# Attention and two dense layers on one core: opening transposes on TensorE, a third buffer for weight pieces, empty rows added behind the second tile of keys

## The chip, the cores and the metric

The kernel runs on one core of one Trainium2 chip. The metric is the device time of one execution in microseconds (us), lower is better. Three runs of the kernel before gave a median of 734.42 us (733.02 to 736.55). Engines are named as the profile names them: PE is TensorE (PEld its weight loads), DVE VectorE, ACT ScalarE, POOL GpSimd, SP the engine that issues nearly all DMAs here.

## The reference

```python
# attention: B, H, S, D = 2, 8, 768, 64; 16 clusters a head
q_assign = argmax(q_n @ c_n.T); k_assign = argmax(k_n @ c_n.T)    # q_n, k_n, c_n: normalised rows
mask = q_assign[:, :, :, None] == k_assign[:, :, None, :]
scores = np.where(mask, q @ k.T / sqrt(D), -1e9)
attn = softmax(scores) @ v                          # 16 (batch, head) pairs
x = attn.transpose(0, 2, 1, 3).reshape(1536, 512)
h = x @ w_in;  x = softplus(h) @ w_out              # layer 1: 512 -> 2048 -> 512
h = x @ w_in2; x = leaky_relu(h, 0.01) @ w_out2     # layer 2
```

The weights come as float64 and are decoded on the chip. Products that need more than half precision are split into high and low halves of 16 bits.

## The kernel before

The 16 (batch, head) pairs are called heads 0 to 15, and each has 768 rows in C = 6 tiles of 128. The work of one head is a chain through all engines:

- `load` fetches q and k (two DMAs). `split` makes 16-bit high and low halves: ACT casts into `nq` (L293) and copies (L295), POOL subtracts (L294). The halves in `n1` are then transposed by one DMA from SP into `t` (L297): 12 blocks of 128x128.
- `assign_mm` multiplies `t` with the transposed centroids `ct` (24 small matmuls, L306); `assign_el` finds each row's cluster on DVE (L319 to L325) and ACT writes the one-hot columns beside the data in `nq` (L328, L329). A second DMA transpose from SP makes `tq` of it (L331, 12 blocks).
- `emit_s1` computes all masked scores once for the row maxima: 12 matmuls (L345), each with a DVE maximum (L352). `emit_m` joins the maxima (L359), PE turns them by a diagonal matmul (L366), and ACT copies them into rows 96 to 127 of `tq` (L374).
- `emit_s2` computes the scores again, 2 times 6 pairs of matmuls (L392, L393), ACT exponentiates (L399), POOL makes the low half (L401); `emit_pv` multiplies with v into one PSUM tile `x` (L428, L429, L433, or L415 for the second tile of keys of heads 0 to 7). `emit_empty` adds, with six matmuls of 32 rows (L451) that read `tq` and `svr` (column sums of v, `emit_sv`), what rows without any key of their cluster get. `emit_norm` divides (L470 to L476).

Beside this, `w_piece` loads 512 KB pieces of the layer-1 weights into `st` (L153, two buffers), DVE decodes them in three steps (L140, L143, L146), ACT and DVE make the halves (L162, L163). From head 8 on, layer-1 matmuls (L697, L710) fill PE between the heads; after the attention, from about 315 us, only layer work is left, and layer 2 (L562) ends the program.

A scheduler places the instructions of every engine in one fixed order when the program is built, by priorities (`at_pri`) and its own estimate of times. At run time each engine takes its instructions strictly in that order, so an instruction that waits holds back all that stand behind it on its engine, and SP holds back DMAs in the same way. Buffer counts decide waits too: `BUFS` gives, for each tile name, buffers in the late pool and extra ones for heads 0 to 7. `tq` has 3 and 1, so the transpose into `tq` of head h in the second half waits for the last reader of `tq` of head h-3, which is its `emit_empty`. `behind_tk(h)` puts an instruction behind head h's `tq` transpose on SP.

Of the kernel before, what the change touches and what calls it, by code (L numbers as in the profile page):

```python
# [8 lines left out]
F32 = mybir.dt.float32  # L9
# [15 lines left out]
BUFS = {  # L25
# [4 lines left out]
}  # L30
# [14 lines left out]
FF_PRI, FF_STEP, FF_RATE = 8, 0.25, 0.75  # L45

W_FREE, W_FROM, W_TO, W_PER = 4, 8, 10, 5
W_PRI = ((0, 0.5), (17, 0.3))
# [8 lines left out]
def attn_moe_kernel(  # L57
# [93 lines left out]
    def w_piece(dsth, dstl, src):  # L151
        st = wst.tile([128, 512, 2], I32, tag="st", name="st")
        nc.sync.dma_start(out=st, in_=src.rearrange("p (n t) -> p n t", t=2))  # L153

        def conv(bank=False):
            if bank:
                c = pm.tile([128, 512], I32, tag="m0", name="wcp")
            else:
                c = wst.tile([128, 512], I32, tag="wc", name="wc")
            decode(c, st)  # L160
            cf = c.bitcast(F32)
            S.activation(out=dsth, in_=cf, func=AF.Copy, scale=WS)  # L162
            V.scalar_tensor_tensor(out=dstl, in0=cf, scalar=WS, in1=dsth, op0=ALU.mult, op1=ALU.subtract)  # L163

        return conv
# [117 lines left out]
    def split_v(h):  # L283
        vv, v2 = v_t.pop(h), v2s[h % V_BUFS]
        S.copy(out=v2[:, :, D:2 * D], in_=vv)
        ENG[by_group(VLO, h)].tensor_tensor(out=v2[:, :, 0:D], in0=vv, in1=v2[:, :, D:2 * D], op=ALU.subtract)

    def split(h):
        qk = ld_t.pop(h)
        n_ = n_of[h]  # L290
        n1 = atile([128, C, 4, D], F16, "n1", h)
        for t_ in range(2):
            S.copy(out=n_[:, t_, :, 0:D], in_=qk[:, t_])  # L293
            G.tensor_tensor(out=n1[:, :, 1 + t_, :], in0=qk[:, t_], in1=n_[:, t_, :, 0:D], op=ALU.subtract)  # L294
            S.copy(out=n1[:, :, 3 * t_, :], in_=n_[:, t_, :, 0:D])  # L295
        t = atile([128, 2 * C, 128], F16, "t1", h)
        nc.sync.dma_start_transpose(out=t, in_=n1.rearrange("p c s d -> p (c s d)"))  # L297
        tp1[h] = t
# [15 lines left out]
    def assign_el(h):  # L314
# [15 lines left out]
        t = atile([128, 2, C, 128], F16, "tq", h)  # L330
        tki[h] = nc.sync.dma_start_transpose(  # L331
            out=t.rearrange("p t c r -> p (t c) r"), in_=n_.rearrange("p t c d -> p (t c d)")
        )
        tp2[h] = t[:, 0], t[:, 1]
# [71 lines left out]
    def emit_pv(h, kt):  # L406
# [5 lines left out]
        if pl is None:  # L412
            pf = p.rearrange("p a r -> p (a r)")
            for c in range(C):
                PE.matmul(  # L415
                    out=xps[:, c * XW:(c + 1) * XW],
                    lhsT=pf[:, c * 128:(c + 1) * 128],
                    rhs=v32s[h % V_BUFS][:, kt, :],
                    start=(kt == 0 and c == 0),
                    stop=False,  # L420
                )
            return
# [7 lines left out]
        for c in range(C):  # L430
            cs = slice(c * 128, (c + 1) * 128)
            o = xps[:, c * XW:(c + 1) * XW]
            PE.matmul(out=o, lhsT=pl[:, cs], rhs=v2[:, kt, D:2 * D + 1], start=False, stop=False)  # L433

# [13 lines left out]
    def emit_empty(h):  # L448
        t, r, xps = tpq[h], svs.pop(h), x_t[h]
        for c in range(C):  # L450
            PE.matmul(out=xps[:, c * XW:(c + 1) * XW], lhsT=t[MR:KS2, c, :], rhs=r[MR:KS2, :], start=False, stop=(c == C - 1))  # L451

# [284 lines left out]
    nc.sync.dma_start(out=cn, in_=cen.rearrange("h c d -> (h c) d"))  # L737
    load(0)
    sq = acon.tile([128, D], F32, name="sq")
    ss = acon.tile([128, 4], F32, name="ss")  # L740
    c16 = acon.tile([128, 4, D], F16, name="c16")
    with at_pri(-9):
# [13 lines left out]
        centred = V.tensor_tensor(out=c16[:, 2:4, :], in0=two, in1=c16[:, 0:2, :], op=ALU.subtract)  # L756
        nc.sync.dma_start_transpose(out=ct, in_=c16.rearrange("p s d -> p (s d)"))
    load(1)
# [10 lines left out]
    for v2 in v2s:  # L769
        G.memset(v2[:, :, 2 * D:2 * D + 1], 1.0)  # L770
    G.memset(ones, 1.0)
    G.affine_select(
        out=ident, in_=ones, pattern=[[1, 128]], compare_op=ALU.is_equal, fill=0.0, base=0, channel_multiplier=-1
    )
    G.memset(ones[:, MR:MR + C], 0.0)
# [119 lines left out]

    def chain(h):
        if h < NH:
            with at_pri(h - LEAD_SPLIT):
                split(h)
            with at_pri(h - LEAD_ASSIGN):  # L900
                assign_mm(h)
                assign_el(h)
            with at_pri(h - LEAD_MAX):
                for c in range(C):
                    emit_s1(h, c)
            if h + 2 < NH:
                with at_pri(h - LEAD_LOAD):
                    load(h + 2)
# [8 lines left out]
    st = {"credit": 0.0}  # L917
    for h in range(AHEAD):
        chain(h)
    split_v(0)  # L920
    for h in range(NH):
# [14 lines left out]
        for j in range(C):  # L936
            with at_pri(h + j / 6):
                emit_s2(h, j)
                if j:
                    emit_pv(h, j - 1)  # L940
            if h < H - 1 and (j + h * C) % W_PER == 0:
                w_step()
# [4 lines left out]
        with at_pri(h + 1):  # L947
            emit_pv(h, C - 1)
            emit_empty(h)
        with at_pri(h + 1 - LEAD_NORM):  # L950
# [50 lines left out]
```

## Time and profile before

| | us |
|---|---|
| median of 3 runs (device time) | 734.42 |
| the profiled execution, device time | 732.15 |
| its span in the trace | 730.4 |
| PE busy / DVE / ACT / POOL in it | 677.0 / 517.3 / 410.9 / 402.5 |
| idle time of PE before its first matmul | 11.72 |

The profile names an instruction by its line, engine, operation and tiles (`tq<-nq` reads `nq` and writes `tq`). Busy time is the union of an engine's instructions. What ended a wait is shown behind an arrow: `<-DMA tq<-nq` is the landing of that DMA. SP's rows (SPq) show how long the issue of a DMA took there, not the transfer. The granted clock of PE is a share of full speed (1.00 is 2.4 GHz, 0.50 is 1.2 GHz).

### The profile page before, as it was taken

The page shows a single profiled execution, that of the slowest core. Times are in us where ns is not written, and L with a number is a line of the kernel's source. Part 1 is how long each engine was busy: PE and PEld are TensorE (multiplying, and loading weights), DVE is VectorE, ACT ScalarE, POOL GpSimd, SP SyncE. Part 2 cuts the span into 40 slices and gives each one's busy share as a digit, 9 for nine tenths or more (in the row PEclk, how much of TensorE's full clock was granted, in tenths as well). Part 3 has the DMA queues.
Part 4 walks back from the last instruction along what each step waited for, and adds up shares of the span by engine and source line. Part 5 has one row for each costly group of instructions (what it writes and reads, how often), then busy time and mean ns, then how long its engine had stood idle before and what let it go on. Part 6 is the DMA issues. An engine that isn't in the chain of part 4 may idle for free. (4 is left out here: it accounts for less than half of the span.)

```text
span 730.4 us, 18968 instructions
## 1 busy us (share of the span) xinstructions
PE 677.0 (93%) x7584; PEld 506.7 (69%) x7584; DVE 517.3 (71%) x1167; ACT 410.9 (56%) x1087; POOL 402.5 (55%) x494
## 2 busy tenths in 40 slices
PE   1798899998889899999999999999999999999997
PEld 1367677665656566656666566558999999999996
DVE  4797798998898782069787867965585757575545
ACT  5476666768878753355245425526555555565553
POOL 6387777778888864303324233325556465565653
PEclk9999999999999999999999999999999999999999
DMA  8985966766565632013322355787000000000000
GB/s 204 221 173 113 181 136 122 170 123 173 129 161 152 141 116 53 2 35 103 110 93 82 108 175 193 235 304 261 3 31 2 30 2 7 27 2 31 2 31 30
DMA packets 104521, 77.87 MB, mean 107 GB/s; under 512 B 78320, under 2 KB 92656, under 8 KB 104432
## 3 DMA queue, kind: packets, MB, share of 16 engines
q1 hardware_dynamic: 104288, 76.40, 40.4%
q8 instruction: 59, 0.97, 0.5%
q14 instruction: 30, 0.25, 0.1%
q10 hardware_dynamic: 144, 0.26, 0.1%
HBM read 50.36 MB, written 10.49 MB: 83 GB/s over the span
## 5 line engine op out<-in xcount | busy, mean ns | idle before, releaser
L401 POOL TENSOR_TENSOR pl<-p 128x768 f16<-128x768 f32 x88 | 128.3, 1468 | 56.3 <-ACT p L399 36.0
L352 DVE TENSOR_REDUCE mm<-s 128x1 f32<-128x384 f32 x190 | 100.6, 548 | 19.3 <-PE s L345 16.7
L562 PEld LDWEIGHTS <-w_in2h 128*128 128x128 f16 x1344 | 98.2, 98 | 5.3 <-issue 0.7
L570 DVE TENSOR_TENSOR gl<-r,gh 128x384 f16<-128x384 f32 (+1 forms) x96 | 63.2, 659 | 50.0 <-ACT gh L608 49.3
L697 PE MATMUL m<-xt,w_inh 128*128 128x384 f16 x512 | 93.8, 326 | 4.2 <-ACT rl L521 3.4
L399 ACT ACTIVATE p<-s 128x384 f32<-128x384 f32 x160 | 74.2, 492 | 30.9 <-PE s L393 28.3
L710 PE MATMUL m<-g_l,w_outh 128*128 128x384 f16 x256 | 83.4, 326 | 2.0 <-DVE g_l L511 1.9
L710 PE MATMUL m<-g_h,w_outh 128*128 128x384 f16 x256 | 83.5, 326 | 0.0
L710 PE MATMUL m<-g_h,w_outl 128*128 128x384 f16 x256 | 83.3, 326 | 0.0
L570 POOL TENSOR_TENSOR r<-r,r 128x128 f32<-128x128 f32 x95 | 47.8, 520 | 55.5 <-ACT r L600 55.2
L697 PEld LDWEIGHTS <-w_inh 128*128 128x128 f16 x512 | 49.7, 98 | 38.7 <-issue 6.1
L608 ACT CAST gh<-r 128x384 f16<-128x384 f32 (+1 forms) x96 | 54.2, 565 | 36.6 <-POOL r L570 33.6
L710 PEld LDWEIGHTS <-w_outh 128*128 128x128 f16 x512 | 49.8, 98 | 32.5
L345 PE MATMUL s<-tq 128*128 128x384 f16 x190 | 62.0, 345 | 9.3 <-DMA tq<-nq 4.5
L562 PEld LDWEIGHTS <-gh 128*128 128x128 f16 x672 | 60.5, 98 | 6.4 <-issue 1.1
L200 POOL TENSOR_TENSOR wd<-wd 128x256 f32<-128x256 f32 x32 | 29.3, 925 | 53.9 <-DVE sg L194 39.2
L562 PE MATMUL i<-xt,w_in2h 128*128 128x128 f16 x576 | 57.2, 219 | 0.1
L392 PE MATMUL s<-t 128*128 128x384 f16 x160 | 53.2, 333 | 3.1 <-ACT p L399 2.3
L393 PE MATMUL s<-tq 128*128 128x384 f16 x160 | 53.2, 333 | 1.6 <-ACT tq L374 1.6
L562 PE MATMUL i<-sh,w_in2h 128*128 128x128 f16 x384 | 53.5, 219 | 0.4 <-ACT r L600 0.4
L562 PE MATMUL i<-sl,w_in2h 128*128 128x128 f16 x384 | 53.5, 219 | 0.0
L562 PE MATMUL i<-sh,w_in2l 128*128 128x128 f16 x384 | 53.4, 219 | 0.0
(145 smaller groups left out, 1861.1 us busy)
## 6 DMA issues: line engine op xcount, KB each, us to landing
st<-in_moe_w_in_dram SPq DMA_DIRECT2D x32, 512.0 KB, 4.6
st<-in_moe_w_out_dram SPq DMA_DIRECT2D x32, 512.0 KB, 3.7
kept<-sg SPq DMA_DIRECT2D x16, 256.0 KB, 2.8
qk<-in_q_dram SPq DMA_DIRECT2D x16, 192.0 KB, 3.5
qk<-in_k_dram SPq DMA_DIRECT2D x16, 192.0 KB, 3.7
v<-in_v_dram SPq DMA_DIRECT2D x16, 192.0 KB, 4.7
kept<-sg SPq DMA_DIRECT2D x24, 128.0 KB, 2.7
out_dram<-ob SPq DMA_DIRECT2D x11, 256.0 KB, 2.0
```

Of the source, the lines that this page charges most:

```text
L200: G.tensor_tensor(out=out, in0=in0, in1=in1, op=ALU.subtract)
L345: PE.matmul(out=o, lhsT=t[:, c, :], rhs=tk[:, 3 * j:3 * j + 3, :], start=True, stop=True,)
L352: V.reduce_max(out=mms[h % 2][:, c, j:j + 1], in_=bank[:, 0:3 * 128], axis=AX)
L392: PE.matmul(out=o, lhsT=t1[:, kt, 1, :], rhs=t1[:, 3 * j:3 * j + 3, 0, :], start=True, stop=False)
L393: PE.matmul(out=o, lhsT=t2[:, kt, :], rhs=tqh[:, 3 * j:3 * j + 3, :], start=False, stop=True)
L399: S.activation(out=p[:, j, :], in_=sp, func=AF.Exp, scale=scale)
L401: G.tensor_tensor(out=pl, in0=p, in1=pb, op=ALU.subtract)
L562: one = PE.matmul(out=bank, lhsT=w_, rhs=x_, start=(first and i == 0), stop=(i == len(ops) - 1), skip_group_check=True)
L570: eng.tensor_tensor(out=out, in0=in0, in1=in1, op=op)
L608: S.copy(out=gh[:, lo:hi], in_=r[:, lo:hi])
L697: PE.matmul(out=hp, lhsT=w_, rhs=x_, start=(i == 0), stop=(i == len(ops) - 1))
L710: PE.matmul(out=yp, lhsT=w_[:, kk, ms], rhs=g_[:, kk, :], start=(n == 0), stop=(n == 3 * KFF - 1))
```

## The change

1. The transposes of `ct`, of `t` for heads 0 and 1, and of `tq` for head 0 are done by PE: matmuls of each 128x128 block against `ident`, up to four to a PSUM bank, copied out by ACT and DVE in turn. In the program these are 38 matmuls, 7 ACT casts and 3 DVE casts more, and 4 DMA transposes fewer. `ident` is made at the beginning.
2. The first two heads are written stage by stage instead of head by head, and on SP the `t` transposes of heads 3 and 4 and the loads of those heads stand behind `tq` transposes of earlier heads.
3. Weight pieces of layer 1 get a third `st` buffer, in the attention's pool; for it, `t` has one early buffer less (5 in all for heads 0 to 7) and `y` has one buffer instead of two.
4. `emit_empty(h)` stands behind the second tile of keys instead of behind the last (with the flags that close the accumulation moved to the last tile's matmuls).

```diff
-    "qk": (2, 1), "n1": (1, 2), "t1": (4, 2), "tq": (3, 1),
+    "qk": (2, 1), "n1": (1, 2), "t1": (4, 1), "tq": (3, 1),
...
-    "dd": (2, 0), "y": (2, 0), "xn": (2, 0),
+    "dd": (2, 0), "y": (1, 0), "xn": (2, 0),
...
+EMPTY_AT = 2
+PE_HEADS = 1
+OPENING = (3, 4)
+ST_MORE = 1
...
     def w_piece(dsth, dstl, src):
-        st = wst.tile([128, 512, 2], I32, tag="st", name="st")
+        n = turn["st"] = (turn.get("st", -1) + 1) % (2 + ST_MORE)
+        st = (wst if n < 2 else at).tile([128, 512, 2], I32, tag="st", name="st", bufs=2 if n < 2 else ST_MORE)
...
+    def pe_transpose(out, in_, blocks, odd=False):
+
+        for i in range(0, blocks, 4):
+            m = min(4, blocks - i)
+            if odd and i == 8:
+                bank = pm.tile([128, 512], F32, tag="m0", name="m")
+            else:
+                bank = ring("as" if blocks <= 4 else "s1" if odd else "s2", 0)
+            for j in range(m):
+                cs = slice((i + j) * 128, (i + j + 1) * 128)
+                PE.matmul(out=bank[:, j * 128:(j + 1) * 128], lhsT=in_[:, cs], rhs=ident, start=True, stop=True)
+            to = out[:, i:i + m].rearrange("p i r -> p (i r)")
+            if i % 8 == 0:
+                S.copy(out=to, in_=bank[:, 0:m * 128])
+            else:
+                V.tensor_copy(out=to, in_=bank[:, 0:m * 128])
...
-        nc.sync.dma_start_transpose(out=t, in_=n1.rearrange("p c s d -> p (c s d)"))
+        if h <= PE_HEADS:
+            pe_transpose(t, n1.rearrange("p c s d -> p (c s d)"), 2 * C, h == 1)
+        else:
+            with behind_tk(h - 2 if h in OPENING else -1):
+                nc.sync.dma_start_transpose(out=t, in_=n1.rearrange("p c s d -> p (c s d)"))
...
+        if h < PE_HEADS:
+            pe_transpose(to, from_, 2 * C)
+        else:
+            tki[h] = nc.sync.dma_start_transpose(out=to, in_=from_)
...
-        nc.sync.dma_start_transpose(out=ct, in_=c16.rearrange("p s d -> p (s d)"))
+        pe_transpose(ct, c16.rearrange("p s d -> p (s d)"), 2)
...
-                with at_pri(h - LEAD_LOAD):
+            if h + 2 < NH and "m" in parts:
+                with at_pri(h - LEAD_LOAD), behind_tk(h - 1 if h + 1 in OPENING else -1):
                     load(h + 2)
...
-    for h in range(AHEAD):
-        chain(h)
+    for parts in "sam":
+        for h in range(AHEAD):
+            chain(h, parts)
...
                 if j:
                     emit_pv(h, j - 1)
+                if j == EMPTY_AT:
+                    emit_empty(h)
...
             emit_pv(h, C - 1)
-            emit_empty(h)
```

Three places show what the new order does. The first is SP from the centroids' transpose on (before), where `t` and `tq` are the outputs of the two DMA transposes of a head and `qk` its loads:

```order
L757 DMA_TRANSPOSE ct<-c_112 128x2x128
L297 DMA_TRANSPOSE t_176<-n_169 128x12x128
L297 DMA_TRANSPOSE t_261<-n_254 128x12x128
L273 DMA qk<-in_q_dram 128x384
L274 DMA qk<-in_k_dram 128x384
L297 DMA_TRANSPOSE t_360<-n_353 128x12x128
L273 DMA qk<-in_q_dram 128x384
L274 DMA qk<-in_k_dram 128x384
L331 DMA_TRANSPOSE tq<-nq_85 128x12x128
L297 DMA_TRANSPOSE t_662<-n_655 128x12x128
L331 DMA_TRANSPOSE tq<-nq_86 128x12x128
```

And the same stretch of SP in the changed kernel, down to the first weight piece:

```order
L323 DMA_TRANSPOSE t_414<-n_407 128x12x128
L361 DMA_TRANSPOSE tq<-nq_86 128x12x128
L278 DMA qk<-in_q_dram 128x384
L279 DMA qk<-in_k_dram 128x384
L323 DMA_TRANSPOSE t_716<-n_709 128x12x128
L278 DMA qk<-in_q_dram 128x384
L279 DMA qk<-in_k_dram 128x384
L278 DMA qk<-in_q_dram 128x384
L279 DMA qk<-in_k_dram 128x384
L361 DMA_TRANSPOSE tq<-nq_87 128x12x128
L158 DMA st<-in_moe_w_in_dram 128x1024
```

Four transposes are gone from the head of the queue; the first weight piece (`st`) still stands behind the `tq` transpose of head 2 (`nq_87`), as it does before.

The second place is DVE ahead of the first decode of a weight piece (`wcp<-st`); `mm_96` are the maxima of head 1 and `as`, `m`, `mx`, `oh` the cluster search, here of head 3. Before:

```order
L359 TENSOR_REDUCE dg_102<-mm_95 128x6
L352 TENSOR_REDUCE mm_96<-s_300 128x1
L361 TENSOR_SCALAR dg_102<-dg_102 128x6x2
L352 TENSOR_REDUCE mm_96<-s_303 128x1
L319 TENSOR_REDUCE mx<-as 128x12
L352 TENSOR_REDUCE mm_96<-s_306 128x1
L320 TENSOR_TENSOR as<-as,mx 128x192
L321 TENSOR_TENSOR as<-as,tab 128x192
L352 TENSOR_REDUCE mm_96<-s_309 128x1
L352 TENSOR_REDUCE mm_96<-s_312 128x1
L323 TENSOR_REDUCE m_693<-as 128x12
L140 TENSOR_SCALAR wcp<-st 128x512
```

The changed kernel at the same place (here `m_445` and `oh` are head 2's):

```order
L349 TENSOR_REDUCE m_445<-as 128x12
L389 TENSOR_SCALAR dg_102<-dg_102 128x6x2
L380 TENSOR_REDUCE mm_96<-s_357 128x1
L351 TENSOR_TENSOR oh<-as,m_445 128x192
L380 TENSOR_REDUCE mm_96<-s_360 128x1
L380 TENSOR_REDUCE mm_96<-s_363 128x1
L475 SCALAR_TENSOR_TENSOR svr<-h_508,sel,as 32x65
L380 TENSOR_REDUCE mm_96<-s_366 128x1
L380 TENSOR_REDUCE mm_96<-s_369 128x1
L380 TENSOR_REDUCE mm_96<-s_372 128x1
L144 TENSOR_SCALAR wcp<-st 128x512
```

Two more maxima of head 1 now stand ahead of the decode, and the cluster search of head 3 stands behind it.

The third place is SP ahead of the `tq` transpose of head 15 (the last `tq` row of each piece). Before:

```order
L331 DMA_TRANSPOSE tq<-nq_85 128x12x128
L280 DMA v_2_94<-in_v_dram 128x6x64
L153 DMA st<-in_moe_w_out_dram 128x1024 x4
L331 DMA_TRANSPOSE tq<-nq_86 128x12x128
L280 DMA v_0_92<-in_v_dram 128x6x64
L454 DMA_TRANSPOSE xt_84<-xn 128x12x128
```

In the changed kernel:

```order
L361 DMA_TRANSPOSE tq<-nq_85 128x12x128
L158 DMA st<-in_moe_w_out_dram 128x1024
L285 DMA v_2_94<-in_v_dram 128x6x64
L158 DMA st<-in_moe_w_out_dram 128x1024 x3
L361 DMA_TRANSPOSE tq<-nq_86 128x12x128
L285 DMA v_0_92<-in_v_dram 128x6x64
L484 DMA_TRANSPOSE xt_84<-xn 128x12x128
```

The order is nearly the same, but the last piece ahead of it is the 27th instead of the 28th, and with three buffers it waits for the decode of the 24th instead of the 26th.

## Rows read from the trace of the kernel before

**Rows 1.** Windows: stretch, its us; busy us (count) of PE, PEld, DVE, ACT, POOL; clock, DMA share, GB/s.

```profile
0.00:30.00 30.00, 10.32 (x126) 5.61 (x127) 17.08 (x64) 14.90 (x38) 15.01 (x33) 1.00 0.92 205
30.00:60.00 30.00, 27.06 (x333) 19.25 (x332) 23.99 (x56) 20.35 (x51) 21.03 (x18) 1.00 0.91 193
160.00:280.00 120.00, 106.97 (x1294) 71.72 (x1291) 97.61 (x201) 90.37 (x218) 95.31 (x84) 0.99 0.59 145
280.00:730.00 450.00, 441.34 (x4466) 341.99 (x4463) 291.86 (x645) 217.04 (x613) 196.93 (x299) 1.00 0.24 77
```

**Rows 2.** Timeline of the opening, all engines: start, us, what, [idle before].

```profile
6.39 0.51 ACT L295 COPY n<-nq 128x384 f16<-128x384 f16 x1
7.87 3.31 SPq L297 DMA_TRANSPOSE t<-n  x2
8.87 0.92 ACT L293 CAST nq<-qk 128x384 f16<-128x384 f32 x2
11.72 0.81 PE L306 MATMUL as<-ct,t 128*128 128x16 f16 x24 [11.72 <-DMA t<-n]
15.82 0.28 ACT L328 ACTIVATE nq<-oh 128x96 f16<-128x96 f16 x1
15.87 0.37 DVE L320 TENSOR_TENSOR as<-as,mx 128x192 f32<-128x192 f32 x1
20.63 1.46 PE L345 MATMUL s<-tq 128*128 128x384 f16 x4 [2.27 <-DMA tq<-nq]
24.03 1.01 DVE L352 TENSOR_REDUCE mm<-s 128x1 f32<-128x384 f32 x2
28.46 0.30 DVE L445 SCALAR_TENSOR_TENSOR svr<-h,sel,as 32x65 f16<-32x65 f16 x1 [0.83 <-ACT h L444]
28.79 0.18 DVE L359 TENSOR_REDUCE dg<-mm 128x6 f16<-128x18 f32 x1
```

**Rows 3.** Groups by form, 30 to 280 us: shapes, count, busy us, mean ns, idle before.

```profile
L162 ACT ACTIVATE w_inh<-wcp 128x512 f16<-128x512 f32 x16 | 9.6, 598 | 3.1 <-DVE wcp L146 3.1
```

**Rows 4.** Timeline of PE, 11 to 40 us.

```profile
29.89 0.84 PE L366 MATMUL s<-ident,dg 128*128 128x128 f16 x6
```

**Rows 5.** Timeline of SP and of DVE around the first weight piece.

```profile
27.74 1.44 SPq L331 DMA_TRANSPOSE tq<-nq  x1
29.23 0.88 SPq L153 DMA_DIRECT2D st<-in_moe_w_in_dram  x1
...
35.00 0.69 DVE L140 TENSOR_SCALAR wcp<-st 128x512 int32<-128x512 int32 x1 [2.32 <-DMA st<-in_moe_w_in_dram]
...
44.56 0.17 DVE L359 TENSOR_REDUCE dg<-mm 128x6 f16<-128x18 f32 x1
```

**Rows 6.** The page's DMA issues: count, KB each, median us from issue to landing.

```profile
st<-in_moe_w_in_dram SPq DMA_DIRECT2D x32, 512.0 KB, 4.6
```

**Rows 7.** Waits of SP (whole span) and DVE (30 to 285): total us, times, longest.

```profile
SPq L331 <- PE x L451: 28.2, 8, 8.0
...
DVE wcp L140 <- DMA st<-in_moe_w_in_dram: 7.2, 3, 3.2
```

**Rows 8.** Timelines of PE and SP around the tq transpose of head 15.

```profile
233.76 0.32 PE L393 MATMUL s<-tq 128*128 128x384 f16 x1
...
228.59 14.27 SPq L153 DMA_DIRECT2D st<-in_moe_w_out_dram  x4
...
244.29 0.35 PE L451 MATMUL x<-svr,tq 32*128 32x65 f16 x6
...
244.72 1.46 SPq L331 DMA_TRANSPOSE tq<-nq  x1
...
250.18 0.50 PE L345 MATMUL s<-tq 128*128 128x384 f16 x2 [1.92 <-DMA tq<-nq]
```

**Rows 9.** Windows of 1 us behind that wait; three in a row read this clock.

```profile
252.00:253.00 1.00, 1.00 (x18) 0.87 (x16) 0.18 (x1) 0.97 (x3) 1.00 (x2) 0.50 0.70 270
```

**Rows 10.** Timeline of PE at head 13's cluster matmuls.

```profile
182.08 0.48 PE L306 MATMUL as<-ct,t 128*128 128x16 f16 x13 [1.22 <-DMA t<-n]
```

More of the change, by code (lines that the diff above doesn't have):

```diff
@@ L330, in assign_el @@
         t = atile([128, 2, C, 128], F16, "tq", h)
-        tki[h] = nc.sync.dma_start_transpose(
-            out=t.rearrange("p t c r -> p (t c) r"), in_=n_.rearrange("p t c d -> p (t c d)")
-        )
+        to, from_ = t.rearrange("p t c r -> p (t c) r"), n_.rearrange("p t c d -> p (t c d)")
+        if h < PE_HEADS:
+            pe_transpose(to, from_, 2 * C)
+        else:
+            tki[h] = nc.sync.dma_start_transpose(out=to, in_=from_)
         tp2[h] = t[:, 0], t[:, 1]
@@ L419, in emit_pv @@
                     start=(kt == 0 and c == 0),
-                    stop=False,
+                    stop=(kt == C - 1 and c == C - 1),
                 )
@@ L432, in emit_pv @@
             o = xps[:, c * XW:(c + 1) * XW]
-            PE.matmul(out=o, lhsT=pl[:, cs], rhs=v2[:, kt, D:2 * D + 1], start=False, stop=False)
+            PE.matmul(
+                out=o, lhsT=pl[:, cs], rhs=v2[:, kt, D:2 * D + 1], start=False, stop=(kt == C - 1 and c == C - 1)
+            )
     def emit_sv(h):
@@ L450, in emit_empty @@
         for c in range(C):
-            PE.matmul(out=xps[:, c * XW:(c + 1) * XW], lhsT=t[MR:KS2, c, :], rhs=r[MR:KS2, :], start=False, stop=(c == C - 1))
+            PE.matmul(out=xps[:, c * XW:(c + 1) * XW], lhsT=t[MR:KS2, c, :], rhs=r[MR:KS2, :], start=False, stop=False)
     def emit_out(b, hh, xn):
@@ L738, in attn_moe_kernel @@
     load(0)
+    G.memset(ones, 1.0)
+    G.affine_select(
+        out=ident, in_=ones, pattern=[[1, 128]], compare_op=ALU.is_equal, fill=0.0, base=0, channel_multiplier=-1
+    )
     sq = acon.tile([128, D], F32, name="sq")
@@ L770, in attn_moe_kernel @@
         G.memset(v2[:, :, 2 * D:2 * D + 1], 1.0)
[L771 to L774, printed above, removed]
     G.memset(ones[:, MR:MR + C], 0.0)
@@ L894, in attn_moe_kernel, with chain @@
     ff = m_steps(moe1())
-    def chain(h):
+    def chain(h, parts="sam"):
         if h < NH:
[L898 to L906, printed above, removed]
-                with at_pri(h - LEAD_LOAD):
+            if "s" in parts:
+                with at_pri(h - LEAD_SPLIT):
+                    split(h)
+            if "a" in parts:
+                with at_pri(h - LEAD_ASSIGN):
+                    assign_mm(h)
+                    assign_el(h)
+            if "m" in parts:
+                with at_pri(h - LEAD_MAX):
+                    for c in range(C):
+                        emit_s1(h, c)
+            if h + 2 < NH and "m" in parts:
+                with at_pri(h - LEAD_LOAD), behind_tk(h - 1 if h + 1 in OPENING else -1):
                     load(h + 2)
```

## The prediction

> **What bounds the kernel now.** Read the windows first [rows 1]: PE, busy 677.0 of 730.4 us by the table, leaves three kinds of idle time. In the first 30 us it idles 19.7 us, from 160 to 280 us 13.0 us, and in the 450 us from 280 on 8.7 us. From 280 us on PE sets the pace, and the change leaves that part's work as it is, so whatever brings the attention to its end sooner is kept to the end. Then the timeline of the opening [rows 2]: PE's first matmul waits until 11.72 us for a DMA transpose, and the score matmuls of head 0 start at 20.63 us, again behind one. Two `t` transposes hold SP for 3.31 us. Third, the waits [rows 7]: SP waits 28.2 us with a `tq` transpose for `emit_empty` (L451), and DVE 7.2 us for weight pieces. Last, head 15 [rows 8, 9]: its `tq` transpose is issued at 244.72, right behind the empty rows of head 12, PE idles 1.92 us until 250.18, and then the granted clock reads 0.50 (1.2 GHz) in three windows of 1 us, from full level before: 1.5 us lost besides the wait.
>
> **Part 1, the opening.** ACT sets the pace of the new opening. Six ACT instructions of 384 columns start from 6.39 to 8.87 us, 0.41 us each [rows 2]. PE's nearest row for a transpose is L366, six 128x128 matmuls against `ident` in 0.84 us, 0.14 each [rows 4]; the nearest for copying out a bank is L162 on ACT, 0.60 us [rows 3], and on DVE a step of 128x512, 0.69 us [rows 5]. The inputs of `t` of head 0 are complete at 6.90 (6.39 + 0.51); PE needs up to 1.7 us for twelve blocks. In the changed order ACT issues six instructions from that copy on before the first cast of `t`: 6.39 + 6 x 0.41 = 8.85; two casts end at 10.05, where the DMA gave 11.72. Then come nine of 0.41 and the two casts of head 1's `t`, 4.9 us, to 14.95, and only then head 0's one-hot columns (before: 15.82), 0.46, to 15.4. Twelve transposes, 1.7, and a last cast, 0.6: the scores of head 0 start at 17.7 instead of 20.63, 2.9 us earlier. `svr` with its wait (0.30 + 0.83) no longer stands ahead of head 0's maximum, so L359 comes at 24.7 instead of 28.79, 4.1 earlier. The 38 matmuls (5.3 us at 0.14) lie in PE's idle 19.7 us; without that cover they would cost 5.3. The DVE casts lie where DVE idles too (17.1 of 30 us busy) [rows 1].
>
> What is late next is the **first weight piece**. On SP it stands behind head 2's `tq` transpose in both orders [rows 5]. That waits for head 2's one-hot: in the changed order five DVE instructions behind L359 (two maxima of 0.5, two search steps of 0.37 and a small one [rows 2]) and three on ACT of 0.2 to 0.5, to about 27.5; its issue takes 1.44, so the piece is issued at 29.0 instead of 29.23. It takes 5.8 us to land here, 4.6 in the median [rows 5, 6]: 33.6 to 34.8, taken as 34.2, only 0.8 us earlier than 35.00. DVE then waits for it some 4 us instead of 2.32, and behind it stand maxima that PE needs. By then DVE has done two maxima more (1.0) but four search steps less (1.5): DVE alone gains 0.8 - 0.5 = 0.3. PE and ACT meanwhile go on with head 0's scores, whose operands were ready 4 us sooner. From there to head 1's maximum took 35.00 to 44.56, 9.6 us [rows 5]; the changed order has two decode steps and two maxima less (2.4), and four search steps more, with `svr` behind instead of ahead (1.5 - 0.6): 8.1, to 42.3, 2.3 us earlier, 1.4 us of it decode steps put off. So the term lies between 0.3 and 4.1; I take **2.3**, the value at head 1's maximum, since DVE idles 6.0 us in 30 to 60 us [rows 1] and can catch up with what is put off.
>
> At PE's price a rule can be weighed. The row gives 0.14 us for one transpose [rows 4]. The Trainium skill, "TensorE: Matmul & The Clock Gate", Part 4 (PE-mode transpose), gives about 275 ns in one kernel's context. By its figure the twelve blocks would take an estimated 3.3 us; what that does is rival C.
>
> **Part 2, empty rows.** Six matmuls move from the end of a head to behind its second tile of keys: no work more or less. What they need, `svr` and L374's rows, is made ahead of the head's first score pair, so PE waits for nothing new there. The gain is that `tq` is free at the head's last score matmul: for head 12 at 234.1 (233.76 + 0.32) instead of 244.6 [rows 8]. SP must reach that transpose in time too. Before, it issues four weight pieces until 242.86 (228.59 + 14.27, 3.6 each), held by decodes; with three buffers the last of them waits for two decodes fewer, 7.1 us at that pace, 235.7. So both parts are needed, and the transpose could go near 236. But the order also puts head 15's first score matmul sooner behind head 12's last: 36 small matmuls (0.06 each by L451's six in 0.35), six of L366 and two score pairs come between, 3 us or a little more of PE's work, where the transpose took 5.4 us to land (244.72 to 250.18). A wait can come again. Full gain 1.92 + 1.5 = 3.4; none if it comes back. I take half, **1.7**.
>
> **Part 3, third buffer.** It lets SP pass a weight piece that waits for a decode. Head 13's `t` came 1.22 us late at 182.08, from an SP that stood behind such pieces [rows 10]; the shortest of DVE's three waits for pieces (7.2 less twice up to 3.2, so 0.8 or more; I take 1.7 as its bound [rows 7]) goes with it. Upper bound 1.2 + 1.7 = 2.9; these waits are on two engines that wait for each other, so I take **1.1**. For the buffer, `t` has five instead of six: head 5's transpose now waits for head 0's last score matmul, and behind it SP holds head 3's `tq`, a load of v and the third piece. By my walk that piece lands near 49.5 and DVE comes to it at 50 to 51: nothing, or at most 1.0 us. `y` with one buffer costs nothing: its next write is a whole head later. The moved loads and `t` transposes of heads 3 and 4 stand on SP ahead of a transpose that waits for ACT anyway.
>
> **Sum.** 2.3 + 1.7 + 1.1 = 5.1 us less. The profiled execution took 732.15 us, 2.27 below the median of 734.42: 732.15 - 5.1 = 727.05, in terms of the median **729.3 us**.
>
> **Rivals.**
>
> A. The weight piece eats the opening: DVE sets the pace of the first heads and the opening keeps 0.3, part 2's wait comes back whole (0), part 3 gives 1.1: 734.42 - 1.4 = 733.0. For: DVE waits longer for the piece than before. Against: DVE's 6.0 us of idle time in 30 to 60 us [rows 1]. Chance 0.27.
>
> B. All upper bounds hold: 4.1 + 3.4 + 2.9 = 10.4, 724.0. For: 13.0 us of PE idle from 160 to 280 us [rows 1] and 28.2 us of SP waiting for empty rows [rows 7]. Against: a wait taken from one engine mostly shows up on the next. Chance 0.15.
>
> C. A transpose on PE costs twice the row. Twelve take 3.3 instead of 1.7 us; the first set is partly hidden behind ACT, and head 0's scores come some 2 us later than reckoned, so that the opening, with the piece behind it, gives nothing: 734.42 - 2.9 = 731.5. The row of L366 speaks against it. Chance 0.03.
>
> D. Slower. Score matmuls stand so soon behind the last scores of the head three before that their `tq` transpose has not landed; PE waits ahead of heads 14 and 15. Price: two waits of 1.92 and two drops of the clock of 1.5, 6.8, where there was one of each: 3.4 lost, and 1.0 with the third piece late. With the opening at 0.3 that is 4.1 us slower, 738.5. It decides once the landing takes longer than the work that lies between, by some 2 us. For: 5.4 us against 3 at head 15. Against: that landing had a load and another transpose beside it. Chance 0.07.
>
> The forecast has 0.48, with 726 to 731.5 as its own range.
>
> **How the numbers follow.** A measurement of this kernel tells about 0.5%, 3.7 us, from no change. Faster by more: most of the forecast (0.41 of 0.48), B, and a little of A: 0.59. Slower by more: most of D, 0.05. Within: 0.36. The range reaches from B's value to A's with no gain but the opening's least: 724.0 to 734.1. It leaves out D and some of B's far side.
>
> **What would show it.** In the changed profile: head 0's score matmuls near 17.7 us and its L359 near 24.7 (part 1); DVE idle some 4 us for the first piece until near 34 (with under 2 the opening gives more); the `tq` transpose of head 15 issued before 240 and no clock of 0.50 behind it (part 2); PE not waiting for head 13's `t` (part 3). I would be wrong if the weight conversions, which move back relative to the heads, become the bound before 280 us, or if the new order opens a wait that this trace cannot show.

## The result, and the profile after

The changed kernel takes 742.0 us (median of 6 runs, 739.71 to 749.57); the kernel before, run beside it, 734.1 us. The ratio is 1.0124 with a 95% interval of 1.0094 to 1.0154: 9 us slower (7.9 by the two medians), where 5 us faster was forecast. The profiled execution spans 739.7 us, that of before 730.4.

The windows of the changed kernel, to be read beside [rows 1] (stretch, its us; busy us and count of PE, PEld, DVE, ACT, POOL; clock, DMA share, GB/s):

```profile
0.00:30.00 30.00, 17.76 (x169) 11.12 (x170) 21.34 (x71) 18.74 (x46) 14.15 (x32) 1.00 0.66 156
30.00:60.00 30.00, 24.31 (x329) 17.45 (x327) 23.88 (x53) 19.99 (x51) 21.55 (x19) 0.94 0.86 180
60.00:160.00 100.00, 87.06 (x1253) 63.01 (x1251) 80.65 (x187) 60.54 (x150) 69.28 (x58) 0.97 0.73 137
160.00:280.00 120.00, 105.25 (x1327) 70.85 (x1325) 102.38 (x211) 93.36 (x224) 95.08 (x85) 1.00 0.58 139
280.00:500.00 220.00, 215.71 (x1481) 131.43 (x1480) 147.22 (x263) 92.52 (x204) 70.13 (x56) 1.00 0.40 125
500.00:740.00 240.00, 233.27 (x3075) 215.58 (x3073) 148.13 (x388) 129.31 (x421) 131.76 (x247) 1.00 0.10 36
```

The stretch from 60 to 160 us, which [rows 1] leaves out, in the kernel before:

```profile
60.00:160.00 100.00, 91.32 (x1374) 68.12 (x1373) 86.73 (x203) 68.28 (x169) 74.25 (x62) 1.00 0.68 138
```

The opening does what it was meant to: PE turns head 0's maxima 4.4 us sooner than at 29.89 [rows 4]:

```profile
25.45 0.82 PE L394 MATMUL s<-ident,dg 128*128 128x128 f16 x6 [0.47 <-DVE dg L389]
```

Then the lead goes, and more: the same step comes 0.7 us sooner than before for head 1, 0.7 later for head 2 and 8.8 later for head 9. PE idles 5.7 + 12.9 + 14.8 = 33.4 us from 30 to 280 us; before it was 2.9 + 8.7 + 13.0 = 24.7. The clock reads 0.50 for three stretches of 3.4 us, from 39.6, 66.9 and 155.6 us, where before there was one (250.7), besides a last one at the very end of each. The spans differ by 9.3 us, and PE's idle and busy time make this up within rounding: idle 7.4 less up to 30 us, 8.7 more from 30 to 280, 1.7 more behind; busy 6.4 more (677.0 to 683.4), of which the added transposes are 5.1. That leaves 1.3 us of busy time for the clock, where half of the 6.8 us more at 0.50 would be 3.4. So most of the loss lies in the heads, not in what follows them.

The longest waits of PE in the changed kernel (total us, times, longest):

```profile
PE as L332 <- DMA t<-n: 6.8, 5, 1.9
PE s L373 <- DVE mm L380: 6.0, 11, 1.8
...
PE s L373 <- DMA tq<-nq: 4.8, 3, 2.3
PE s L420 <- ACT p L427: 4.0, 8, 1.2
...
PE m L420 <- ACT p L427: 2.9, 3, 2.0
```

`t` makes PE wait 6.8 us, all behind 110 us; in the kernel before it was 2.8 from 30 us on (the rest was the opening's 11.72). `tq` makes it wait 4.8 instead of 2.3 from 30 us on.

**Two places in detail.** ACT, PE and the windows of 1 us around 38 us:

```profile
37.57 0.51 ACT L315 CAST nq<-qk 128x384 f16<-128x384 f32 x1 [3.02 <-DMA qk<-in_q_dram]
37.99 0.48 ACT L427 ACTIVATE p<-m 128x384 f32<-128x384 f32 x1
```

```profile
38.52 0.32 PE L420 MATMUL m<-t 128*128 128x384 f16 x1 [1.97 <-ACT p L427]
```

```profile
38.00:39.00 1.00, 0.48 (x7) 0.34 (x7) 0.01 (x1) 1.00 (x4) 0.84 (x1) 1.00 0.62 129
39.00:40.00 1.00, 0.36 (x8) 0.10 (x4) 1.00 (x2) 1.00 (x3) 0.64 (x2) 0.80 2.34 216
40.00:41.00 1.00, 0.78 (x8) 0.61 (x9) 1.00 (x4) 1.00 (x4) 1.00 (x2) 0.50 0.08 13
```

ACT stands 3.02 us at the cast of a later head, whose load (issued at 35.43) has not come; the exponential that PE needs is queued behind that cast; PE idles 1.97 us and is busy for 0.84 of the 3 us up to 40.00; its clock falls to half at 39.6, until 43.0. Near 155 us PE waits for `t` itself. SP, and the window in which the clock falls:

```profile
143.86 1.32 SPq L158 DMA_DIRECT2D st<-in_moe_w_in_dram  x2
145.27 0.57 SPq L285 DMA_DIRECT2D v<-in_v_dram  x1
146.46 0.33 SPq L158 DMA_DIRECT2D st<-in_moe_w_in_dram  x1
146.88 3.76 SPq L323 DMA_TRANSPOSE t<-n  x1
```

```profile
155.30:160.00 4.70, 4.70 (x83) 3.85 (x84) 2.93 (x7) 2.67 (x6) 4.58 (x5) 0.64 0.38 105
```

Three pieces of 512 KB go out in 3 us, and the `t` transpose behind them lands 8.3 us after its issue (4.3 for the one issued at 150.59 in the kernel before, with no piece close ahead of it); PE waits 1.91 us for it.

### The profile page after: what moved, and what is told of

Its sections match the earlier page's. It is cut to its first block, busy times and chain, and to the rows that moved or that the text cites. A ratio compares the mean times of both kernels' runs of the same rounds, so it can differ in the third digit from the quotient of the medians.

```text
span 739.7 us, 19053 instructions
## 1 busy us (share of the span) xinstructions
PE 683.4 (92%) x7622; PEld 509.4 (69%) x7622; DVE 523.6 (71%) x1170; ACT 414.5 (56%) x1094; POOL 402.0 (54%) x494
```

## The experiments

Ratios are to the kernel before, run beside each on the same chip; a difference in us is the difference of two ratios times 734. The columns on the right come from one profiled execution of each kernel: "idle" is PE's idle time from 30 to 280 us, "half" the time at a clock of 0.50 between 39 and 600 us. It leaves out the stretches at 0.50 between 23 and 39 us, which several kernels have, old opening or new (10.2 us in only_empty, pay_t, order_b and seven_t, none in before), and the one at the end. The clock also varies between executions of one kernel: its mean was 0.986 to 1.000 in the 29 of the kernel before beside pay_t, and 0.977 to 0.992 in the 9 of pay_t.

| kernel | `t` buffers | piece buffers | opening | empty rows | ratio (95%) | idle | half |
|---|---|---|---|---|---|---|---|
| before | 6 | 2 | old | end | 1 | 24.7 | 3.4 |
| changed | 5 | 3 | new | tile 2 | 1.0124 (1.0094 to 1.0154) | 33.4 | 10.2 |
| only_opening | 6 | 2 | new | end | 0.9956 (0.9934 to 0.9978) | 28.4 | 6.8 |
| only_empty | 6 | 2 | old | tile 2 | 1.0013 (0.9987 to 1.0038) | 24.4 | 3.4 |
| only_third | 5 | 3 | old | end | 1.0089 (1.0058 to 1.0120) | 29.1 | 10.2 |
| no_third | 6 | 2 | new | tile 2 | 1.0025 (0.9998 to 1.0053) | 29.6 | 3.4 |
| no_opening | 5 | 3 | old | tile 2 | 1.0066 (1.0040 to 1.0092) | 29.6 | 10.2 |
| no_empty | 5 | 3 | new | end | 0.9977 (0.9949 to 1.0004) | 29.1 | 3.4 |
| empty_last | 5 | 3 | new | tile 5 | 1.0142 (1.0102 to 1.0182) | 33.1 | 10.2 |
| empty_split | 5 | 3 | new | tile 2 and end | 1.0054 (1.0032 to 1.0076) | 27.4 | 6.8 |
| pay_t | 5 | 2 | old | end | 1.0083 (1.0055 to 1.0111) | 27.4 | 20.5 |
| pay_t_opening_empty | 5 | 2 | new | tile 2 | 1.0073 (1.0041 to 1.0104) | 30.9 | 20.5 |
| third_paid_by_p | 6 (`p` 4) | 3 | new | tile 2 | 0.9998 (0.9968 to 1.0027) | 24.9 | 10.2 |
| third_p_no_empty | 6 (`p` 4) | 3 | new | end | 1.0058 (1.0032 to 1.0084) | 31.7 | 13.7 |
| order_a | 6 | 2 | old | end | 1.0071 (1.0046 to 1.0097) | 27.5 | 6.8 |
| order_a_five_t | 5 | 2 | old | end | 1.0218 (1.0192 to 1.0245) | 32.0 | 27.3 |
| order_b | 6 | 2 | old | end | 0.9992 (0.9971 to 1.0012) | 24.6 | 0.0 |
| order_b_five_t | 5 | 2 | old | end | 1.0088 (1.0064 to 1.0113) | 27.7 | 17.1 |
| seven_t | 7 (`p` 4) | 2 | old | end | 1.0070 (1.0041 to 1.0099) | 28.0 | 10.2 |
| opening_seven_t | 7 (`p` 4) | 2 | new | end | 1.0000 (0.9976 to 1.0024) | 31.3 | 10.2 |

**Each part alone, and each part undone.** The edits are the switches of the change and its buffer table; undoing the third buffer gives back what was paid for it:

```diff
-    "qk": (2, 1), "n1": (1, 2), "t1": (4, 1), "tq": (3, 1),
+    "qk": (2, 1), "n1": (1, 2), "t1": (4, 2), "tq": (3, 1),
-    "dd": (2, 0), "y": (1, 0), "xn": (2, 0),
+    "dd": (2, 0), "y": (2, 0), "xn": (2, 0),
-ST_MORE = 1
+ST_MORE = 0
```

> The change without its third piece buffer: two buffers for weight pieces, six for `t`, two for `y` as in the kernel before; opening and empty rows as changed. Theory T (the price of the buffer): with five buffers instead of six a `t` transpose waits for the scores of the head five before, holds SP, and `t` lands late; PE's waits for `t` behind the opening, 6.8 us in five places in the changed kernel against 2.5 in the kernel before, and the clock drop behind the one at 155.25, make most of the 9 us. It expects 733 to 736 us here, and under 3 us of waits for `t`. Theory O (the opening): the loads and `t` transposes put back by the new opening reach ACT late, PE waits behind it and the clock drops twice before 70 us; it expects 740 to 743 here, the waits for `t` being a consequence. Theory M (the mix: each part moves the order of all engines, and no part is the cause by itself) expects 735 to 741.

> The change without its opening: all transposes of the first heads by DMA, written head by head, loads not put back; third buffer and empty rows as changed. Theory O expects 732 to 735 us, with no clock drop before 70 us, since the opening's lead of 4.0 us at 30 us is lost by 70 us to waits behind ACT's loads and two clock drops. Theory T expects 741 to 745: the lead of the opening is missing too, and the waits for `t` stay at 6 us or more. Theory M: 735 to 742.

> The change with the rows of empty tiles at the head's end again; opening and third buffer as changed. Theories T and O: within 3 us of the changed kernel, 739 to 745, since neither has to do with the empty rows; SP waits some 25 us for the empty rows again, as before. A theory E (the scores of head h+3 come too soon behind those of head h, so PE waits for `tq`: 4.8 us between 160 and 280 us against 2.4 before) expects 735 to 738.

> The kernel before with the new opening alone: transposes of the first heads by TensorE, stage by stage, loads and `t` transposes of heads 3 and 4 put back; two piece buffers, six `t`, empty rows at the end. Theory O expects 738 to 742 us. Theory T expects 730 to 733: the opening keeps 1 to 4 us of its lead. Theory M: 732 to 738.

> The kernel before with the empty rows behind the second tile of keys, and nothing else: opening by DMA, two piece buffers, six `t`. The empty rows added 5.0 us where the new opening stood alone (from a ratio of 0.9956 to 1.0025) and 10.8 where the buffer was there too. If their price is their own (theory E), this is 738 to 742 us against 735 of the kernel before. If it comes only from meeting the new opening or the buffer (theory M), it is 733 to 737.

> The kernel before with the third piece buffer, paid for by one `t` and one `y`, and nothing else. With the new opening the buffer cost 1.5 us (0.9956 to 0.9977), with opening and empty rows 7.3. Theory T (the lost `t` buffer costs by itself) expects 736 to 740 us; if it costs only where the empty rows pull the work of later heads forward, 733 to 736.

Alone, the opening gains 0.44% (3.2 us), the empty rows change nothing that can be measured, and the third buffer with its payment costs 0.89% (6.5 us). With 1.0 for the empty rows, which is within the noise, these add up to 4.3 us, under half of the 9. Theory O falls with only_opening, theory E with only_empty; theory M's ranges hold no_third, no_opening, only_opening and only_empty, and no_empty lies below what any theory expected. Undone, things look otherwise: without the move of the empty rows the changed kernel is 10.8 us faster, the largest step of all, though that move alone costs nothing; beside the third buffer without the opening it is worth -1.7, beside the opening without the third buffer +5.1. The opening's sign changes too: -3.2 alone, -8.2 beside the third buffer, +0.9 beside the empty rows, +4.3 beside both. Only the third buffer with its payment has the same sign in all four surroundings: +6.5 alone, +1.5 with the opening (within the noise), +3.9 with the empty rows, +7.3 with both.

**Is it where the empty rows stand, or what they set free?**

```diff
-EMPTY_AT = 2
+EMPTY_AT = 5
```

In the split kernel five of a head's six rows stay behind tile 2 and the sixth goes to the end, so that `tq` is held as before.

> The changed kernel with the empty rows behind the sixth tile of keys (after the last scores, ahead of the head's last value matmuls) instead of the second; their stop flags as in the change. `tq` is read by the scores of all six tiles, so it comes free at the same point as in the change, within some 1.5 us. Theory R (it is the earlier release of `tq` that costs: transposes and score matmuls of head h+3 are drawn forward, and PE stands behind DVE's maxima and behind late `t`) expects 740 to 744 us, as the change. Theory P (it is the place of the rows: `svr` and the rows of L402 are wanted sooner) expects 733 to 736, as without the move.

> The changed kernel with five of the six empty-row matmuls behind the second tile of keys, and the sixth at the head's end, as in the kernel before. The rows stand as early as in the change, but `tq` is held to the head's end. Theory R expects 733 to 737 us, as the changed kernel without the move (734). Theory P expects 740 to 744. If both this and the run with the rows behind the sixth tile lie between, or both on one side, the cost hangs on neither but on which order the build happens to find.

Rows later, with `tq` free just as early: 1.0142 (744.6 us), just above theory R's range. `tq` held again: 1.0054, between the bounds of both theories. The early release is no gain; that it is the cause is not shown by one pair, as the order runs below make plain.

**The payment without the buffer, the buffer without the payment.** `pay_t` changes one number of the kernel before:

```diff
-    "t1": (4, 2),
+    "t1": (4, 1),
```

The other two take the room from the early heads' exponentials, `"p": (3, 1)` for `(3, 2)`, and leave `t` at six.

> The kernel before with five buffers for `t` instead of six and nothing else: still two piece buffers, two `y`. In every kernel so far with five, the transposes of `t` of heads 5 to 9 are issued about one head later (heads 5, 6, 7 at 44.8, 53.5, 68.4 us with the third piece buffer alone, at 31.5, 44.6, 52.6 before). Theory T (the lost `t` buffer is the price; the piece buffer itself is nearly neutral) expects what the third piece buffer alone gave, 738 to 742 us against 734, with the same late transposes. Theory B (the third piece buffer itself costs: two pieces issued back to back, their conversions bunched) expects 733 to 736.

> The changed kernel with two piece buffers and two `y`, but still five buffers for `t`; opening and empty rows as changed. Theory T: 741 to 745 us, as the changed kernel (743), since it has the price. Theory B: 735 to 739, as the run with opening and empty rows without the third buffer (1.0025).

> The changed kernel with its third piece buffer and six `t`: the room is taken from the exponentials instead (`p` of the early heads with four buffers, not five). Theory T: 734 to 738 us, no later than with opening and empty rows alone, and `t` of heads 5 to 7 issued near 40, 45, 56 again. Theory B: 741 to 745. Should the fourth `p` be what is missed, waits of ACT for POOL's `pl` would rise above 2.5 us.

> The same with the empty rows at the head's end: new opening, third piece buffer paid by `p`, six `t`. Theory T: the opening's gain stays and the buffer costs nothing, 730 to 733 us (ratio 0.993 to 0.997). Theory B: 734 to 737, the opening's gain lost to the buffer as in the run with opening and third buffer.

Giving a `t` buffer away costs 6.1 us without getting anything for it, as much as the third buffer with its whole payment (6.5). In the change's own surroundings it costs less: with the new opening and the moved empty rows, five `t` instead of six are worth 3.5 us (no_third to pay_t_opening_empty, kernels that differ in this number alone), and the third piece buffer with the single `y` adds 3.7 more. With the room taken from `p` the changed kernel keeps all three of its parts and is level with the kernel before (0.9998); the 9 us are gone. Theory B's ranges miss all four runs, but that a third piece buffer costs nothing is shown only in the old opening (pay_t to only_third, 0.4 us). The last run missed theory T's range as well: 1.0058 where at most 0.997 was expected. It is no_empty with six `t` and four `p` instead of five and five, and 5.9 us slower.

How the missing buffer acts can be read in `pay_t`. Its timeline of SP, the `t` transposes of heads 5 to 9:

```profile
45.12 1.46 SPq L323 DMA_TRANSPOSE t<-n  x1
53.00 2.49 SPq L323 DMA_TRANSPOSE t<-n  x1
70.59 1.47 SPq L323 DMA_TRANSPOSE t<-n  x1
91.28 3.40 SPq L323 DMA_TRANSPOSE t<-n  x1
115.00 1.44 SPq L323 DMA_TRANSPOSE t<-n  x1
```

The same five in the kernel before:

```profile
31.52 3.71 SPq L297 DMA_TRANSPOSE t<-n  x1
44.61 2.27 SPq L297 DMA_TRANSPOSE t<-n  x1
52.58 2.60 SPq L297 DMA_TRANSPOSE t<-n  x1
78.23 1.44 SPq L297 DMA_TRANSPOSE t<-n  x1
87.01 3.21 SPq L297 DMA_TRANSPOSE t<-n  x1
```

Each line of the upper list stands about where the next head's stands in the lower (within 0.6 us for the first two, within 9 for the others): five transposes in a row come about one head later. With five buffers those of heads 5 to 8 wait for the last scores of the head five before, where with six head 5 waited for none and heads 6 to 8 for those of the head six before; only from head 10 on are the rings alike. What follows from the one issued at 91.28, on ACT and on PE of `pay_t`:

```profile
98.29 0.92 ACT L317 COPY n<-nq 128x384 f16<-128x384 f16 x2 [2.19 <-DMA t<-n]
99.12 0.48 ACT L427 ACTIVATE p<-m 128x384 f32<-128x384 f32 x1
```

```profile
99.66 0.32 PE L420 MATMUL m<-t 128*128 128x384 f16 x1 [2.31 <-ACT p L427]
```

```profile
100.00:101.00 1.00, 1.00 (x5) 0.51 (x4) 0.00 (x0) 0.97 (x3) 1.00 (x3) 0.61 0.00 0
101.00:102.00 1.00, 1.00 (x5) 0.45 (x3) 0.56 (x1) 0.59 (x2) 1.00 (x1) 0.50 0.72 201
```

The transpose lands 7.0 us after its issue. Until then it reads `n`, into which ACT wants to copy a later head; behind that copy stand the exponentials that PE waits for; behind PE's wait the clock falls. So this wait of PE's is laid to `p`, not to `t`. Two others name `t` (3.5 us together from 30 to 285 us, 2.8 in the kernel before). And the longest from 60 to 100 us goes by SP's queue. There the `t` transpose issued at 70.59 keeps SP from 62.94 on; behind it stands a `tq` transpose, which reads the `nq` that ACT wants next. On SP, ACT and PE:

```profile
72.59 1.43 SPq L361 DMA_TRANSPOSE tq<-nq  x1
77.97 0.93 ACT L315 CAST nq<-qk 128x384 f16<-128x384 f32 x2 [5.40 <-DMA tq<-nq]
79.55 0.32 PE L421 MATMUL m<-tq 128*128 128x384 f16 x1 [2.89 <-ACT tq L402]
```

In the kernel before ACT waits 2.80 us for a `tq` at 75.43, and PE does not stand behind it. SP's row in the waits tells of `n` from the other side: its loads wait for POOL's `n`

```profile
SPq L278 <- POOL n L316: 33.0, 9, 6.4
```

in the changed kernel, 12.1 us in five waits in the kernel before, 23.3 in seven in `pay_t`.

**How much is order alone worth?** The empty rows' changing sign and the missed run asked for it. Nothing changes here but a number that the scheduler sorts by; buffers and instructions stay:

```diff
-        with at_pri(h + j / 6):
+        with at_pri(h + j / 6 + 0.01):
```

(`- 0.01` in the second order), each with six and with five `t`.

> The kernel before with nothing but another order: the priority of each tile of scores is put back by 0.01 of a head. Buffers, transposes, empty rows and all instructions' work as before; about one in seven of DVE's and ACT's instructions stands in another place, about as many as the move of the empty rows displaces. Theory S (order alone moves the time by several us, so that the signs of the opening and of the empty rows, which changed with what else was in the kernel, are no property of these parts): a time off that of before by 2 to 8 us, either way. Theory P (order alone is worth under 2 us, so the differences between the runs belong to the parts): 732 to 737 us.

> The same order change with five buffers for `t` instead of six. Theory T (the lost `t` buffer costs, whatever the order): 4 to 9 us above the run with the order change and six `t`. If the price came only by the accident of the order in the kernels measured so far, the two lie within 3 us, or the other way.

> The kernel before with the priority of each tile of scores put forward by 0.01 of a head, and nothing else: a smaller change of order, about one in thirty of DVE's and ACT's instructions. Theory S: up to 4 us off the kernel before, either way. Theory P: within 2 us.

> That order with five buffers for `t`. Theory T: 4 to 9 us above the run with this order and six `t`. Otherwise within 3 us of it, or below.

The first order alone costs 0.71% (5.2 us), the second nothing. So differences of up to some 5 us between two of these kernels need not belong to the part by which they differ, and theory P falls. With the old opening the `t` buffer stands above that: its pairs cost 6.1 us in the old order, 10.8 in the first new one (above the 4 to 9 expected) and 7.0 in the second. The 3.5 us in the change's own surroundings do not stand above it, though the sign is the same in all four pairs. The windows from 60 to 100 us, with six and with five: before and `pay_t`,

```profile
60.00:100.00 40.00, 36.12 (x574) 28.09 (x574) 32.25 (x79) 25.95 (x66) 30.18 (x25) 1.00 0.75 145
```

```profile
60.00:100.00 40.00, 32.26 (x403) 22.49 (x403) 28.15 (x68) 23.05 (x57) 22.91 (x19) 0.87 0.51 109
```

then the second order with six and with five:

```profile
60.00:100.00 40.00, 36.87 (x596) 28.59 (x593) 32.34 (x78) 26.82 (x67) 30.50 (x25) 1.00 0.70 150
```

```profile
60.00:100.00 40.00, 31.87 (x410) 22.19 (x409) 28.61 (x69) 23.67 (x58) 24.32 (x21) 0.94 0.52 111
```

The pairs repeat each other: nearly a third fewer matmuls in these 40 us (PE busy 11 and 14% less), less work on every engine, and a clock that falls where it had stayed at full level. With the new opening and the moved empty rows this picture is absent; no_third and pay_t_opening_empty, with six and with five:

```profile
60.00:100.00 40.00, 36.96 (x542) 27.37 (x540) 35.30 (x84) 26.25 (x66) 28.90 (x24) 1.00 0.75 147
60.00:100.00 40.00, 36.76 (x570) 27.49 (x568) 31.79 (x76) 26.23 (x66) 29.86 (x26) 1.00 0.74 131
```

So how the missing buffer acts was read in kernels with the old opening, and is not shown for the changed kernel itself.

**The other way round.** Seven `t`, paid by `p`:

> The kernel before with seven buffers for `t` in the early heads instead of six, the room taken from `p` (four early buffers, not five); nothing else. If SP's wait for a free `t` is what five buffers lengthen, a seventh shortens it: `t` of heads 6 to 8 issued at least 5 us sooner than 44.6, 52.6, 78.2. Whether that pays is open: theory T with the wait still binding at six gives 729 to 732 us; if six are enough, 733 to 737, and order alone can move either by some 5 us.

> The same with the new opening: transposes of the first heads by TensorE, stage by stage; seven `t`, four early `p`, two piece buffers, empty rows at the end. The opening alone gave 0.9956. If a seventh `t` pays, 728 to 731 us; if six are enough, 731 to 736.

`t` of heads 6 to 8 does come sooner in seven_t (40.8, 48.2, 61.4 us: by 3.8, 4.4 and 16.9, where 5 was expected of each), but the times are 1.0070 and 1.0000: worse than with six and five `p`. Whether that is the price of the `p` buffer or of the order, these runs don't tell apart; the two kernels with six `t` and four `p` don't settle it either. The fastest kernel measured is only_opening: the new opening and nothing else, faster than both kernels, by 0.44% against the one before (no_empty, 0.9977, is within the noise of it).

## Why the prediction was wrong

**Part 1, the opening: right in itself.** Forecast were head 0's scores at 17.7 us, L359 (now L387) at 24.7, the first piece at 34.2 and head 1's maximum at 42.3. The changed kernel's rows on PE and DVE:

```profile
16.92 1.12 PE L373 MATMUL s<-tq 128*128 128x384 f16 x3 [0.67 <-ACT tq L306]
```

```profile
23.82 0.17 DVE L387 TENSOR_REDUCE dg<-mm 128x6 f16<-128x18 f32 x1
33.14 0.70 DVE L144 TENSOR_SCALAR wcp<-st 128x512 int32<-128x512 int32 x1 [2.21 <-DMA st<-in_moe_w_in_dram]
42.20 0.17 DVE L387 TENSOR_REDUCE dg<-mm 128x6 f16<-128x18 f32 x1
```

All are within about a microsecond (DVE waited 2.21 us for the piece where some 4 were forecast), and alone the opening gains 3.2 us where 2.3 was taken; beside the other two parts it costs 4.3. What failed is that the lead was carried to the end as a term of a sum: in the changed kernel head 2's maximum is at 56.79 us, against 56.39 before, and on the way there lie ACT's wait for a load and the half clock behind it (above). That wait is one of ACT's order: with the opening alone the same load is issued at nearly the same time, 35.14, but exponentials stand ahead of the cast, ACT waits at most 1.43 us between 30 and 50 us, and head 2's maximum is at 53.6. So it seems that the same opening keeps its lead or loses it by where the scheduler puts one cast; no run moves that cast alone.

PE's price was right too. A set of twelve transposes of `tq` takes 1.46 us in the trace:

```profile
14.78 1.04 PE L303 MATMUL s<-ident,nq 128*128 128x128 f16 x8 [1.00 <-ACT nq L354]
15.61 0.63 PE L303 MATMUL m<-ident,nq 128*128 128x128 f16 x4
```

That is 0.12 us each, 0.14 by [rows 4], so rival C is out (its sum has a slip: 1.7 and 1.1 are 2.8, not 2.9). One alone lasts 0.31 us by its record, but they overlap. The 275 ns that the Trainium skill gives ("TensorE: Matmul & The Clock Gate", Part 4) are for TensorE's transpose mode in one kernel; for these plain matmuls against `ident` they are not the pace.

**Part 2, the empty rows: no gain.** 1.7 us was taken; alone the move is worth -0.13% to +0.38% in time, and in the other surroundings between -1.7 and +10.8 us. SP no longer waits for the empty rows, but head 15's `tq` transpose is issued at 249.10, not near 236, since the heads are by then behind and SP waits for other things. PE waits 1.75 us for it (1.92 in [rows 8]), this time without a fall of the clock. The step "both parts are needed, and the transpose could go near 236" reckoned with SP's queue of before and one wait removed.

**Part 3, the third buffer: the mis-sized term.** Beside the other two parts it costs 7.3 us where a gain of 1.1 was taken. The gain that was looked for is there in part: DVE's waits for weight pieces fall from 7.2 us [rows 7] to 3.8. The price is what failed: "nothing, or at most 1.0" for the `t` buffer, where four pairs give 3.5 to 10.8 us, the 3.5 in the change's own surroundings. The prediction followed head 5's transpose and what SP held behind it, the queue, for one head. It did not follow the next four transposes, each of which loses a head as well, nor the tile that they read: in `pay_t` `n` is kept from ACT and POOL, ACT's copy holds up exponentials, and PE stands. One such wait of about 2 us can cost more than its length: the half clock behind it adds up to 1.7.

**Rivals and range.** The sign is that of D, but not its mechanism: PE waits 4.8 us for `tq` (heads 13 to 15), no clock falls behind these waits, and with the `t` buffer given back (and one `p` taken) 9 us come back while the empty rows stay moved. Of D's price the 2.5 us more of `tq` waits are there, and putting the rows back alone gives 10.8 us (no_empty), so the moved rows are not cleared either. Weight conversions as the bound, named as what would make the forecast wrong, do not show: none of PE's waits in the changed kernel is for a converted weight. The range had no room for order: a change that moves one in seven instructions on DVE and ACT is, by one of the two order runs, worth 5 us without any reason that the diff names.

**What stays open.** Step by step from the kernel before to the changed one, by only_opening, no_third and pay_t_opening_empty, the parts are worth -3.2 (opening), +5.1 (empty rows), +3.5 (five `t`) and +3.7 us (third piece buffer with one `y`): 9.1 in all. In another sequence, by pay_t, only_third and no_empty, they are +6.1 (five `t`), +0.4 (piece buffer), -8.2 (opening) and +10.8 (empty rows). So what a part costs depends on what stands beside it. Alone the parts give 4.3 of the 9 us; the rest is of the size of order alone, with waits that can be pointed at (155 us, three pieces ahead of `t`), but no run makes it the property of one part. That holds for the empty rows' 10.8 us too.

## What to carry to other kernels

When a buffer is given away to pay for another, follow every later user of its ring until the rings agree again, and for each not only who waits for the tile but what its producer reads: that is freed late too, and what waits for it may stand in an in-order queue ahead of something else entirely. Test the payment alone, and again beside the rest of the change: it is one number in a table, and its price here was 6.1 us in one place and 3.5 in the other. Where a scheduler writes the order, run the kernel with a meaningless change of priority before giving a difference of half a per cent to any part, and compare parts in pairs over several orders.

## What the runs showed of the hardware

The clock was part of the differences, but less than the time at 0.50 suggests. From the kernel before to `pay_t` the profiled spans differ by 12.3 us (730.4 to 742.7, the slowest execution of `pay_t`): PE idles 5.9 us more and is busy 6.4 us more, with 26.2 us more at 0.50 (10.2 of them from 28.5 us on). For the first order with five `t` it is 10.3 and 8.8 of 19.1 us, with 24.9 us more at 0.50. The Trainium skill ("TensorE: Matmul & The Clock Gate", Terms) puts the penalty at the throttled time times one minus the granted share, half of it here: an estimate of 13.1 and 12.4 us. PE's busy time grew by less, so in these traces that half is an upper bound. Where PE is full, half of the time is indeed lost: neighbouring matmuls of 384 columns in `pay_t` start 0.16 us apart at full clock (99.66 and 99.82) and 0.32 apart at half (100.48 and 100.80).

The clock fell behind waits of 1.91, 1.97 and 2.31 us, but not behind others of 1.75 (at 253.00 in the changed kernel) and 2.27:

```profile
211.60 0.50 PE L373 MATMUL s<-tq 128*128 128x384 f16 x2 [2.27 <-DMA tq<-nq]
```

So the length of the wait alone doesn't tell.

And a DMA transpose issued behind three pieces of 512 KB took 8.3 us to land, though its issue came only 0.4 us after that of the last of them. The kernel before has such landings too: its four transposes of `t` with a piece issued in the 4 us ahead of them took 5.6 to 8.1 us, its twelve others 3.7 to 5.1.
